# A second scheduling fence per step in the first phase of a fused attention and gated-layer kernel on one Trainium2 core

## The chip, the cores and the metric

The kernel runs on one core of one Trainium2 chip. The metric is the device time of one execution in microseconds (us), as the median of several runs. A core has TensorE (PE in the profile), VectorE (DVE), ScalarE (ACT), GpSimd (POOL) and SyncE (SP), which here issues nearly all DMAs. Each engine takes its instructions strictly in the order in which they were written for it, and waits at the head of its queue until the semaphores that an instruction names have been raised.

## What is computed

Three layers follow one another, over 4 batches of 576 positions:

```python
# 1: 8 heads of 64, causal within a window of 128
scores = q @ k.T / 8 + slope[h] * -|i - j|;  attn = softmax(masked scores);  x = attn @ v      # 576 x 512
# 2: gated layer with a spatial product
h = relu(x @ w_in);  u, v = h[:, :512], h[:, 512:]
v_n = (v - mean(v)) / sqrt(var(v) + 1e-6)
x = (u * (w_spatial @ v_n + b_spatial)) @ w_out
# 3: four causal attention experts of width 64, of which the best two by x @ w_gate are summed with softmaxed gates
```

Products that need more precision than one rounded operand gives are done in three passes over a high and a low part of each operand. The low part is the source less its rounded high part.

## The kernel before

**Two phases.** The first phase (lines 161 to 639) does layer 1 and the parts of layer 2 up to the gate. The second phase (from line 641) folds `w_out` into the weights of layer 3 and does layer 3. The change touches the first phase alone.

**Tiles and steps.** `tiles` (line 527) lists 20 tiles (b, j): batch b and 128 positions j, the fifth of 64. The loop of lines 605 to 635 makes 20 steps, s = 2 to 21; each works on several tiles at different stages. In step s PE makes the attention result `px` of tile s-2 (`attend`, line 402) and the scores of tile s (`scores`, line 341), and then, in pieces between other matmuls, the transposes of the probabilities of tile s-1 (`transposes`, line 383). ACT and DVE make the softmax of tile s (`softmax`, line 359; its exponentials are L151, its reduction L150). Names in this text carry batch and position: `px0_3` is batch 0, position 3.

**The eviction of x.** `take` (line 419) moves `px` from PSUM into the operand x of layer 2: `split` (line 131) rounds it into the high part on ACT (L132) and subtracts on DVE for the low part (L129). The pool `psT` (line 110) holds one buffer, shared by `px` and by the transposes `pt`, so the first transpose of a step has to wait until both halves of that step's eviction have read `px`.

**Work between.** `dense.pull` (line 76) hands PE pieces of layer 2 of earlier tiles: `v_tile` (`pv`, L436), `u_half` (`pu`, L499) and `spatial` (`pg`, L516 and L521). Their followers on ACT and DVE are the ReLU `vr` (L444), its statistics (L447, L448, L462 to L469), the normalisation (L472), the high part `vn0_t` (ACT, L475, and L482 for a half tile) and low part `vn1_t` (DVE, L129). POOL fills the padding of the last `vn0` tile after that (L483). The PSUM pool `psD` has three buffers for these.

**Other work that the loop spreads out.** `late_chunks` (line 549) decodes the last four pieces of `w_in` in steps 2 to 5; its word operations are L281 on ACT and L284 to L289 on DVE. `setup` (line 247) loads and splits the spatial weights in steps 6 to 8: a load into `st_wsp` (two buffers of tag `f64w`), an ACT cast (L254) and a DVE subtraction (L129). `out_weights` (line 291) decodes `w_out` from step 9 on (L281, L284 to L289, L308, cast `ho` L313, low part `lo`). `load_chunk` (line 324) loads q, k and v for two steps ahead; v has five buffers, so a v load waits on SP for the attention that reads the oldest one. After the loop, `load_wcat` (line 666) loads pieces of the third layer's weights into `st_wc`, in the same two buffers of tag `f64w`.

**What sets the order.** PE's order is that of the code, written by hand (line 1059: a manual schedule for PE). The order of ACT, DVE, POOL and SP is chosen while the program is built, by a scheduler with a timeline of its own. The one means that the code has over it is `tc.no_sync_barrier()` (line 608), a fence that no instruction passes in that ordering, on any engine; it emits no instruction and no semaphore. Each step has one, at its head:

```python
        tc.no_sync_barrier()
        if s == 9:
            early_stack.close()
            outw = out_weights(right.enter_context(...))
        if s > 2:
            b, j = tiles[s - 2]
            if j in (0, 2) and b > 0:
                dense.through(f"u{b - 1}_{j // 2}")
            px = attend(b, j)
        if s < len(tiles):
            scores(*tiles[s])
        if s > 2:
            take(*tiles[s - 2], px)
        if 4 <= s + 2 < len(tiles):
            load_chunk(*tiles[s + 2])
        now[0] += 1
        dense.pull(RATE / 6)
        parts(s)
```

The rest of a step (lines 626 to 635) is twice: `transposes`, `dense.pull`, `softmax`, `dense.pull`, `parts`.

Of the kernel before, what the change touches and what calls it, by code (L numbers as in the profile page):

```python
# [102 lines left out]
def block_kernel(ctx, tc, qP, kP, v, w_in, wspT, bsp, w_outT, wcat, wo, rel, relt, low, tri, out):  # L103
# [27 lines left out]
    def split(hi, lo, src):  # L131
        nc.scalar.copy(hi, src)  # L132
        lo_part(lo, src, hi)
# [157 lines left out]
    def out_weights(pool):  # L291

        is64 = w_outT.dtype == I64

        def load(k):
            raw = pool.tile([P, 512], w_outT.dtype, tag="raw", name=f"rawo{k}", bufs=2)
            nc.sync.dma_start(raw, w_outT[k * P : (k + 1) * P, :])
            return raw

        nxt = load(0)  # L300
        yield
        for k in range(4):
            w = nxt
            if is64:
                w = pool.tile([P, 512], F32, tag="w", name=f"wo{k}", bufs=2)
                f = pool.tile([P, 512], F32, tag="f", name=f"fo{k}", bufs=3)
                yield from word_bits(w, f, nxt, f)
                nc.vector.tensor_add(w, w, f)  # L308
            yield
            if k < 3:  # L310
                nxt = load(k + 1)
            hi = pool.tile([P, 512], F32R, tag="f", name=f"ho{k}", bufs=3)
            nc.scalar.copy(hi, w)  # L313
            nc.sync.dma_start(wt_dram[0, k], hi.bitcast(F32))
            yield
            lo = pool.tile([P, 512], F32R, tag="f", name=f"lo{k}", bufs=3)
            lo_part(lo, w, hi)
            nc.sync.dma_start(wt_dram[1, k], lo.bitcast(F32))
            yield
            yield  # L320
# [3 lines left out]
    def load_chunk(b, j):  # L324

        q0, qn = TOK[j]
        Q_[b, j] = a1.tile([P, 4, P], F32, tag="q", name=f"q{b}_{j}", bufs=3)
        nc.sync.dma_start(Q_[b, j], qP[b, :, j])
        if j == 0:
            K_[b] = a1.tile([P, 4, S], F32, tag="k", name=f"k{b}")  # L330
        if b == 0:
            nc.sync.dma_start(K_[b][:, :, q0 : q0 + qn], kP[b, :, :, q0 : q0 + qn])
        elif j == 0:
            nc.sync.dma_start(K_[b], kP[b])
        V_[b, j] = a1.tile([P, 512], F32, tag="v", name=f"v{b}_{j}", bufs=5)
        nc.sync.dma_start(V_[b, j][:qn], v[b, q0 : q0 + qn])
# [4 lines left out]
    def scores(b, j):  # L341

        q0, qn = TOK[j]
        k0 = max(0, q0 - P)
        kn = min(S, q0 + P) - k0
        for g in range(2):
            ps = psS.tile([P, 2, 512], F32, tag="S", name=f"ps{b}_{j}_{g}")
            for h in range(2):
                hp = 2 * g + h
                if j < 4:  # L350
                    for o in range(2):
                        r = slice(64 * o, 64 * o + 64)
                        nc.tensor.matmul(ps[:, o, 256 * h : 256 * h + kn], Q_[b, j][r, hp, :], K_[b][r, hp, k0 : k0 + kn], start=True, stop=True)  # L353
                else:

                    nc.tensor.matmul(ps[:, h, :kn], Q_[b, j][:, hp, :], K_[b][:, hp, k0 : k0 + kn], start=True, stop=True)
            st_[b, j, g] = ps

    def softmax(b, j, g):

        ps = st_[b, j, g]
        p = a1.tile([P, 4, P], F32, tag="p", name=f"p{b}_{j}_{g}", bufs=3)
        st = a1.tile([P, 8], F32, tag="stat", name=f"st{b}_{j}_{g}", bufs=4)
        if j == 4:
            nc.vector.copy_predicated(ps[:, :, 0:64], lowm[:, 128:192].unsqueeze(1).to_broadcast([P, 2, 64]), ps[:, :, 128:192])
            for h in range(2):
                row_softmax(p[:, h, :], ps[:, h, 0:P], reltail[:, 2 * g + h, :], st[:, h : h + 1], st[:, 4 + h : 5 + h])
            n = 2
        else:
            view = ps.rearrange("p o (h c) -> p (o h) c", h=2)  # L370
            if j > 0:
                nc.vector.copy_predicated(view[:, :, 0:P], lowm[:, 0:P].unsqueeze(1).to_broadcast([P, 4, P]), view[:, :, P:256])
            for i in range(4):
                o, h = i // 2, i % 2
                row_softmax(p[:, 2 * h + o, :], view[:, i, 0:P], relm[:, min(j, 1), 2 * (2 * g + h) + o, :], st[:, i : i + 1], st[:, 4 + 2 * h + o : 5 + 2 * h + o])
            n = 4
        sm = st[:, 4 : 4 + n]
        nc.vector.tensor_scalar(sm, sm, 1e-9, None, op0=ALU.add)
        nc.vector.reciprocal(sm, sm)
        nc.vector.tensor_tensor(p[:, :n, :], p[:, :n, :], sm.unsqueeze(2).to_broadcast([P, n, P]), op=ALU.mult)  # L380
        st_[b, j, g] = p

    def transposes(b, j, g):
        p = st_[b, j, g]
        n = 4 if j < 4 else 2
        pt = psT.tile([P, 4, P], F32, tag="T", name=f"pt{b}_{j}_{g}")
        here = a1.tile([P, 4, P], F32, tag="pT", name=f"pT{b}_{j}_{g}", bufs=4)
        before = None
        for i in range(n):
            nc.tensor.transpose(pt[:, i, :], p[:, i, :], ident)  # L390
        nc.scalar.copy(here[:, :n], pt[:, :n])  # L391
        if j > 0:

            before = a1.tile([P, 4, P], F32, tag="pU", name=f"pU{b}_{j}_{g}", bufs=4)
            w = P if j < 4 else 64
            m = 4
            u_, h = (t[:, :n].rearrange("p i (o q) -> p (i o) q", q=w) for t in (before, here))
            nc.gpsimd.affine_select(out=u_, in_=h, pattern=[[0, m], [-1, w]], compare_op=ALU.is_gt, fill=0.0, base=0, channel_multiplier=1)  # L398
            nc.gpsimd.affine_select(out=h[:w], in_=h[:w], pattern=[[0, m], [1, w]], compare_op=ALU.is_ge, fill=0.0, base=0, channel_multiplier=-1)  # L399
        st_[b, j, g] = (before, here)  # L400

    def attend(b, j):

        q0, qn = TOK[j]
        px = psT.tile([P, 4, P], F32, tag="T", name=f"px{b}_{j}")
        for hp in range(4):
            pT = st_[b, j, hp // 2]
            for t, w in ((j - 1, pT[0]), (j, pT[1])):
                if t < 0:
                    continue  # L410
                kb = TOK[t][1]
                for o in range(2):
                    h = 2 * hp + o
                    rhs = w[:, 2 * (hp % 2) + o, :] if j < 4 else w[:kb, hp % 2, 64 * o : 64 * o + 64]
                    nc.tensor.matmul(px[64 * o : 64 * o + 64, hp, :qn], V_[b, t][:kb, h * 64 : h * 64 + 64], rhs,  # L415
                                     start=(t == max(0, j - 1)), stop=(t == j))
        return px

    def take(b, j, px):
        q0, qn = TOK[j]  # L420
        if j < 4:
            split(x[0][:, :, q0 : q0 + P], x[1][:, :, q0 : q0 + P], px)
        else:
            twice = [t[:, :, 512:640].rearrange("p m (r c) -> p m r c", r=2) for t in x]
            split(*twice, px[:, :, :64].unsqueeze(2).to_broadcast([P, 4, 2, 64]))
        xready[b, j] = now[0] + (b == 0)
# [133 lines left out]
    def parts(s):  # L560

        next(late, None)
        for _ in range(2 if 6 <= s < 9 else 0):
            next(prep, None)
        if s >= 9:
            next(outw, None)
# [38 lines left out]
    for s in range(2, len(tiles) + 2):  # L605
        now[0] = 4 * s
# [4 lines that stand above are left out]
            outw = out_weights(right.enter_context(tc.tile_pool(name="later", bufs=1, side="right")))  # L611
# [6 lines that stand above are left out]
            scores(*tiles[s])  # L618
        if s > 2:
            take(*tiles[s - 2], px)  # L620
        if 4 <= s + 2 < len(tiles):
            load_chunk(*tiles[s + 2])
        now[0] += 1
        dense.pull(RATE / 6)
        parts(s)
        for g in range(2):
            if 1 <= s <= len(tiles):
                transposes(*tiles[s - 1], g)
            dense.pull(RATE / 6)
            if s < len(tiles):  # L630
                softmax(*tiles[s], g)
# [4 lines that stand above are left out]
# [427 lines left out]
```

## Time and profile before

| | |
|---|---|
| median of 3 runs | 510.27 us (509.82 to 510.5) |
| span of the profiled execution, first to last instruction | 508.8 us |
| its own time | not listed apart; the median is 1.5 us over its span |
| first phase, up to the last `pg` | 0 to 298 us |
| PE busy | 486.7 us, 96% |
| DVE, ACT, POOL busy | 308.4, 261.3, 98.2 us (61%, 51%, 19%) |
| DMA | 44.34 MB, 87 GB/s over the span |
| mean granted TensorE clock | 0.989 |

A row of the timeline gives the start in us from the span's start, the duration, engine, line, operation and tiles (buffer numbers left out), how many were merged, and in brackets the time that the engine sat idle before it, with what ended that. PEld is PE's loading of weights, beside its matmuls; SPq is SP's issuing of DMAs. A granted clock of 1.00 is 2.4 GHz and 0.50 is 1.2 GHz.

### The profile page before, as it was taken

What the parts mean: (1) busy time and instruction counts of PE and PEld (TensorE: products, weight loads), DVE (VectorE), ACT (ScalarE), POOL (GpSimd) and SP (SyncE); (2) the same over time, 40 slices, a digit from 0 to 9 for tenths busy, and PEclk for the clock granted to TensorE, in tenths of its full rate; (3) what the DMA queues carried; (4) which work ended last, traced back from release to release, by engine and by line L of the source; (5) the groups of instructions that cost most, each with busy time, mean ns of one, the idle gap of its engine ahead of it and who ended that gap; (6) DMA issues with size and microseconds to landing.
All of it is one profiled execution on the core that took longest, in us unless ns stands there. A gap on an engine that the chain in (4) does not pass through costs nothing.

```text
span 508.8 us, 10533 instructions
## 1 busy us (share of the span) xinstructions
PE 486.7 (96%) x3910; PEld 425.1 (84%) x3910; DVE 308.4 (61%) x1069; ACT 261.3 (51%) x778; POOL 98.2 (19%) x205
## 2 busy tenths in 40 slices
PE   8879889999999999999999999999999999999995
PEld 6547668898988988899887999998899899897783
DVE  4978868655787766785463723455484565555431
ACT  4765457533666436473353513355575555545563
POOL 0012210222101222111112010103322243232131
PEclk9999979999999999999999999999999999999999
DMA  8931223215321451201304660311000000002231
GB/s 286 371 133 43 65 87 103 115 69 168 107 95 43 181 191 43 95 2 48 110 1 125 224 204 1 94 63 32 1 22 3 2 22 1 1 1 84 84 104 63
DMA packets 25063, 44.34 MB, mean 87 GB/s; under 512 B 5810, under 2 KB 8242, under 8 KB 24628
## 3 DMA queue, kind: packets, MB, share of 16 engines
q1 hardware_dynamic: 24868, 43.54, 25.3%
q8 instruction: 31, 0.51, 0.4%
q14 instruction: 20, 0.16, 0.1%
q10 hardware_dynamic: 144, 0.13, 0.1%
HBM read 32.13 MB, written 11.53 MB: 86 GB/s over the span
## 4 chain that ended last, share of the span: by engine, by line
PE 77%; DVE 10%; ACT 6%; DMA 4%; issue 1%; SPq 1%; ACTq 0%
PE pg L516 10%; PE pv L436 10%; PE pq L780 10%; PE pu L499 6%; PE pvB L804 6%; PE pxB L906 5%; PE pout L927 5%; PE px L415 4%; PE ptB L888 4%; PE psB L845 4%; PE pw L679 3%; PE ps L353 3%; PE pt L390 2%; ACT p L151 2%; PE pg L521 2%; DMA raw<-in_w_in 2%
## 5 line engine op out<-in xcount | busy, mean ns | idle before, releaser
L151 ACT ACTIVATE p<-p,st 128x128 f32<-128x128 f32 x144 | 56.3, 392 | 37.6 <-DVE st L150 37.6
L436 PE MATMUL pv<-win,x 128*128 128x512 f32 x240 | 64.8, 413 | 0.7 <-ACT x L132 0.7
L780 PE MATMUL pq<-x,W 128*128 128x288 f32 x384 | 58.3, 302 | 0.8 <-DVE k L129 0.8
L516 PE MATMUL pg<-wsp,vn 128*128 128x288 f32 x384 | 58.9, 298 | 0.1
L398 POOL TENSOR_SCALAR_AFFINE_SELECT pU<-pT 128x512 f32<-128x512 f32 (+1 forms) x32 | 22.9, 715 | 168.7 <-ACT pT L391 164.7
L499 PE MATMUL pu<-x,win 128*128 128x288 f32 x384 | 55.2, 298 | 0.0
L780 PEld LDWEIGHTS pq<-x,W 128*128 128x128 f32 x384 | 52.0, 188 | 3.6 <-DVE k L129 1.5
L158 POOL TENSOR_SCALAR pB<-pB,stB 128x128 f32<-128x128 f32 (+4 forms) x72 | 39.1, 562 | 78.8 <-DVE stB L868 62.4
L516 PEld LDWEIGHTS pg<-wsp,vn 128*128 128x128 f32 x384 | 52.9, 188 | 1.3 <-issue 1.0
L499 PEld LDWEIGHTS pu<-x,win 128*128 128x128 f32 x384 | 52.0, 188 | 1.9 <-issue 0.5
L436 PEld LDWEIGHTS pv<-win,x 128*128 128x128 f32 x240 | 44.6, 195 | 10.0 <-issue 1.0
L151 ACT ACTIVATE pB<-pB,stB 128x128 f32<-128x128 f32 (+3 forms) x64 | 35.7, 559 | 21.4 <-DVE stB L150 21.4
L150 DVE CUSTOM_DVE_ANT_0 pB<-psB,trit 128x128 f32<-128x128 f32 (+3 forms) x64 | 28.2, 486 | 9.9 <-PE psB L845 9.2
L804 PE MATMUL pvB<-W,x 128*128 128x260 f32 (+1 forms) x240 | 34.2, 289 | 0.0
L927 PE MATMUL pout<-wo,o 128*128 128x512 f32 x108 | 30.8, 411 | 0.9 <-ACT o L132 0.9
L804 PEld LDWEIGHTS pvB<-W,x 128*128 128x128 f32 (+1 forms) x240 | 29.9, 178 | 1.7 <-issue 1.7
L888 PE MATMUL ptB<-ident,pB 128*128 128x128 f32 (+1 forms) x200 | 30.7, 273 | 0.0
L390 PE MATMUL pt<-ident,p 128*128 128x128 f32 x144 | 23.2, 280 | 7.6 <-DVE x L129 6.0
L150 DVE CUSTOM_DVE_ANT_0 p<-ps,relm 128x128 f32<-128x128 f32 x128 | 29.5, 285 | 0.7 <-DMA relm<-in_rel 0.2
L906 PE MATMUL pxB<-pTB,vt 128*64 128x128 f32 (+2 forms) x480 | 28.3, 262 | 1.4 <-ACT pTB L889 1.4
L415 PE MATMUL px<-pT,v 128*64 128x128 f32 (+1 forms) x320 | 29.4, 274 | 0.3 <-POOL pT L399 0.3
L353 PE MATMUL ps<-k,q 64*128 64x256 f32 (+1 forms) x256 | 28.6, 363 | 0.6 <-DMA k<-in_kP 0.6
(147 smaller groups left out, 875.6 us busy)
## 6 DMA issues: line engine op xcount, KB each, us to landing
q<-in_qP SPq DMA_DIRECT2D x20, 256.0 KB, 2.9
g_dram<-g SPq DMA_DIRECT2D x16, 288.0 KB, 2.1
raw<-in_w_in SPq DMA_DIRECT2D x8, 512.0 KB, 6.8
v<-in_v SPq DMA_DIRECT2D x16, 256.0 KB, 3.4
gf<-g_dram SPq DMA_DIRECT2D x4, 1024.0 KB, 5.5
out<-ot SPq DMA_DIRECT2D x15, 256.0 KB, 2.0
k<-in_kP SPq DMA_DIRECT2D x3, 1152.0 KB, 5.3
rawo<-in_w_outT SPq DMA_DIRECT2D x4, 512.0 KB, 4.2
```

The lines of the kernel that those rows point to most:

```text
L150: nc.vector.tensor_tensor_reduce(s_view, ps_view, tab, -0.125, FLT_MAX, ALU.add, ALU.min, nm)
L151: nc.scalar.activation(s_view, s_view, AF.Exp, bias=nm, scale=-1.0, accum_out=sm)
L353: nc.tensor.matmul(ps[:, o, 256 * h : 256 * h + kn], Q_[b, j][r, hp, :], K_[b][r, hp, k0 : k0 + kn], start=True, stop=True)
L415: nc.tensor.matmul(px[64 * o : 64 * o + 64, hp, :qn], V_[b, t][:kb, h * 64 : h * 64 + 64], rhs, start=(t == max(0, j - 1)), stop=(t == j))
L436: nc.tensor.matmul(pv, x[i][:, k, t0 : t0 + P], win[j][:, k, 512:1024], start=(n == 0), stop=(n == 11))
L499: nc.tensor.matmul(pu[:, :HALF], win[i][:, k, m * P : (m + 1) * P], x[j][:, k, c], start=(n == 0), stop=(n == 11))
L516: nc.tensor.matmul(pg[:, :HALF], vn[i][k][:, m * P : (m + 1) * P], wsp[j][:, k, c], start=(n == 0), stop=False)
L780: nc.tensor.matmul(pq[:, :HALF], W[i][:, k, c0 : c0 + P], G[j][:, k, c], start=(n == 0), stop=(n == 11))
L804: nc.tensor.matmul(pv[:tn, :260], G[i][:, k, COL[t] : COL[t] + tn], W[j][:, k, 512:772], start=(n == 0), stop=(n == 11))
L888: nc.tensor.transpose(pt[:kb, n, :], p[pr][:, o, c0 : c0 + kb], ident)
L906: nc.tensor.matmul(px[64 * o : 64 * o + 64, pr, :qn], vt[:kb, c, (2 * pr + o) * 64 : (2 * pr + o) * 64 + 64], rhs, start=(c == 0), stop=(c ...
L927: nc.tensor.matmul(po[:tn], o2[i][:, pr, :tn], wos[j][:, pr, :], start=(n == 0), stop=(n == 5))
```

## The change

After `take`, a step now has a second fence. What was written before it (the step's attention, scores and eviction of x, and all of earlier steps) can no longer be ordered behind what is written after it (the loads for two steps ahead, the dense pieces' followers, decoding, transposes and softmax), and the other way round.

```diff
@@ -618,6 +618,7 @@
             scores(*tiles[s])
         if s > 2:
             take(*tiles[s - 2], px)
+            tc.no_sync_barrier()
         if 4 <= s + 2 < len(tiles):
             load_chunk(*tiles[s + 2])
         now[0] += 1
```

No instruction is added or removed. PE's and POOL's orders are the same as before, instruction by instruction. DVE's, ACT's and SP's differ, in the first phase and up to the splitting of `st_wc`; the second phase's are the same from the first `pw` on. Line numbers in the orders of the changed kernel are higher by one from line 621 on.

DVE in step 5, from the statistics of `v_tile` to the softmax of tile (1, 0): `vr0_t` is normalised, `vn1_t` is its low part, `x1` the low part of x. Before:

```order
L469 TENSOR_TENSOR vs0_422<-vs0_422 128x3
L472 TENSOR_SCALAR vr0_0_423<-vr0_0_423,vs0_422 128x512
L472 TENSOR_SCALAR vr0_1_572<-vr0_1_572,vs0_422 128x512
L472 TENSOR_SCALAR vr0_2_679<-vr0_2_679,vs0_422 128x512
L129 TENSOR_TENSOR vn1_0_115<-vr0_0_423,vn0_0_110 128x512
L129 TENSOR_TENSOR vn1_1_116<-vr0_1_572,vn0_1_111 128x512
L129 TENSOR_TENSOR vn1_2_117<-vr0_2_679,vn0_2_112 128x512
L129 TENSOR_TENSOR x1_105<-px0_3_702,x0_104 128x4x128
```

And now:

```order
L469 TENSOR_TENSOR vs0_422<-vs0_422 128x3
L472 TENSOR_SCALAR vr0_0_423<-vr0_0_423,vs0_422 128x512
L129 TENSOR_TENSOR x1_105<-px0_3_704,x0_104 128x4x128
L472 TENSOR_SCALAR vr0_1_573<-vr0_1_573,vs0_422 128x512
L472 TENSOR_SCALAR vr0_2_681<-vr0_2_681,vs0_422 128x512
```

The low part of x stands ahead of five operations that stood ahead of it.

SP's DMA issues between steps 5 and 7 (`v1_3` is the v load of tile (1, 3), `st_wsp` the spatial weights). Before:

```order
L328 DMA q1_3_832<-in_qP 128x512
L252 DMA st_wsp0_836<-in_wspT 128x576
L252 DMA st_wsp1_839<-in_wspT 128x576
L336 DMA v1_3_834<-in_v 128x512
L252 DMA st_wsp2_873<-in_wspT 128x576
```

And now:

```order
L328 DMA q1_3_836<-in_qP 128x512
L336 DMA v1_3_838<-in_v 128x512
L252 DMA st_wsp0_840<-in_wspT 128x576
L252 DMA st_wsp1_843<-in_wspT 128x576
L252 DMA st_wsp2_877<-in_wspT 128x576
```

The two first loads of spatial weights went behind the v load. On ACT the cast of `st_wsp0` stands in both kernels right behind the x of `px0_4`, ahead of the exponentials of tile (1, 1).

ACT behind the last tile's eviction, at the end of the first phase. Before:

```order
L132 CAST x0_104<-px3_4_3139 128x4x128
L132 CAST wc00_3279<-st_wc0_3287 128x772
L132 CAST wc01_3280<-st_wc1_3289 128x772
L444 ACTIVATE vr3_4_3171<-pv3_4_3158 128x512
L503 ACTIVATE u0_106<-pu3_0_1_3177 128x288
L462 ACTIVATE vs3_2909<-vs3_2909,eps_81 128x2
L463 ACTIVATE vs3_2909<-vs3_2909 128x2
L503 ACTIVATE u1_107<-pu3_1_1_3197 128x288
L475 CAST vn0_3_113<-vr3_3_3134 128x512
```

And now:

```order
L132 CAST x0_104<-px3_4_3157 128x4x128
L444 ACTIVATE vr3_4_3190<-pv3_4_3177 128x512
L462 ACTIVATE vs3_2925<-vs3_2925,eps_81 128x2
L503 ACTIVATE u0_106<-pu3_0_1_3196 128x288
L463 ACTIVATE vs3_2925<-vs3_2925 128x2
L503 ACTIVATE u1_107<-pu3_1_1_3216 128x288
L132 CAST wc00_3298<-st_wc0_3306 128x772
L475 CAST vn0_3_113<-vr3_3_3152 128x512
```

The cast of `st_wc0` went behind the ReLU pieces and stands right ahead of `vn0_3`. On DVE its subtraction likewise went to just ahead of `vn1_3`. On SP the loads of `st_wc0` and `st_wc1`, which stood ahead of the loads of `trit`, `tritail` and the eight pieces of `wt`, now stand behind these ten.

## Rows read from the trace of the kernel before

**Rows 1.** Who waited for whom, PE: us in total, times, longest us.

```profile
PE pt L390 <- DVE x L129: 6.0, 5, 3.7
```

**Rows 2.** Timeline of PE, step 5 and into step 6: start, us, what, idle before.

```profile
60.88 1.16 PE L353 MATMUL ps<-k,q 64*128 64x128 f32 x16
65.78 0.69 PE L390 MATMUL pt<-ident,p 128*128 128x128 f32 x2 [3.73 <-DVE x L129]
66.12 3.76 PE L436 MATMUL pv<-win,x 128*128 128x512 f32 x8
...
71.70 0.34 PE L415 MATMUL px<-pU,v 128*64 128x64 f32 x4
```

**Rows 3.** Timeline of DVE and ACT, step 5.

```profile
61.86 1.46 DVE L472 TENSOR_SCALAR vr<-vr,vs 128x512 f32<-128x512 f32 x3
...
62.44 1.14 ACT L475 CAST vn<-vr 128x512 fp32r<-128x512 f32 x2 [1.42 <-DVE vr L472]
...
63.23 1.89 DVE L129 TENSOR_TENSOR vn<-vr,vn 128x512 fp32r<-128x512 f32 x3
...
65.04 0.68 DVE L129 TENSOR_TENSOR x<-px,x 128x512 fp32r<-128x512 f32 x1
```

**Rows 4.** Busy time by stretch: PE, PEld, DVE, ACT, POOL, granted clock, DMA share, GB/s.

```profile
33.00:37.20 4.20, 1.44 (x7) 0.63 (x5) 4.20 (x17) 3.33 (x14) 1.55 (x2) 1.00 0.29 120
37.20:40.70 3.50, 2.89 (x28) 2.92 (x30) 3.36 (x10) 1.05 (x3) 1.27 (x2) 0.51 0.00 0
...
64.50:71.40 6.90, 5.62 (x16) 4.44 (x16) 5.02 (x25) 3.91 (x19) 1.32 (x4) 0.51 0.26 92
```

**Rows 5.** The page, part 5: busy us, mean ns of one, then idle before.

```profile
L151 ACT ACTIVATE p<-p,st 128x128 f32<-128x128 f32 x144 | 56.3, 392 | 37.6 <-DVE st L150 37.6
```

**Rows 6.** Timeline of SP's DMA issues, with one row of ACT, steps 5 to 7.

```profile
62.96 0.94 SPq L252 DMA_DIRECT2D st_wsp<-in_wspT  x2
...
73.66 0.33 SPq L336 DMA_DIRECT2D v<-in_v  x1
...
76.53 5.41 SPq L252 DMA_DIRECT2D st_wsp<-in_wspT  x4
...
79.31 0.67 ACT L254 CAST wsp<-st_wsp 128x576 fp32r<-128x576 f32 x1 [0.44 <-DMA st_wsp<-in_wspT]
```

**Rows 7.** Timeline of PE, step 6.

```profile
76.15 2.09 PE L436 MATMUL pv<-win,x 128*128 128x512 f32 x8
78.53 0.65 PE L390 MATMUL pt<-ident,p 128*128 128x128 f32 x4 [0.29 <-ACT pT L391]
```

**Rows 8.** Timeline of DVE, step 10, and of ACT and PE, step 12.

```profile
130.33 0.69 DVE L129 TENSOR_TENSOR x<-px,x 128x512 fp32r<-128x512 f32 x1 [0.52 <-ACT x L132]
...
159.38 0.62 ACT L313 CAST ho<-wo 128x512 fp32r<-128x512 f32 x1 [2.22 <-DVE wo L308]
...
162.79 0.66 PE L390 MATMUL pt<-ident,p 128*128 128x128 f32 x4 [0.63 <-ACT pT L391]
```

**Rows 9.** Timeline of PE, step 20.

```profile
266.20 0.44 PE L390 MATMUL pt<-ident,p 128*128 128x128 f32 x2 [0.89 <-DVE x L129]
```

**Rows 10.** Timeline of all engines, end of the first phase.

```profile
277.55 1.07 SPq L668 DMA_DIRECT2D st_wc<-in_wcat  x2
...
283.13 0.62 POOL L483 TENSOR_SCALAR vn<-pad 33x512 fp32r<-33x512 f32 x1 [9.80 <-DVE vn L129]
283.26 1.74 PE L516 MATMUL pg<-wsp,vn 128*128 128x288 f32 x12
283.63 0.84 ACT L132 CAST wc<-st_wc 128x772 fp32r<-128x772 f32 x1 [0.76 <-DMA st_wc<-in_wcat]
...
284.50 0.96 DVE L129 TENSOR_TENSOR wc<-st_wc,wc 128x772 fp32r<-128x772 f32 x1 [1.53 <-ACT wc L132]
...
284.84 0.43 PE L521 MATMUL pg<-wsp,vn 97*128 97x288 f32 x2
```

**Rows 11.** The page, part 6: DMA issues, KB each, median us from issue to landing.

```profile
st_wc<-in_wcat SPq DMA_DIRECT2D x4, 386.0 KB, 4.9
```

## The prediction

> **What bounds the kernel now.** I read the rows of who waited for whom first, then the timelines around the longest of these waits, then the granted clock by stretch. PE is busy nearly all the time, so what can be won or lost in the first phase is PE's idle time and PE's time at the lower clock. The wait that the change aims at is there: PE's transposes waited 6.0 us in five places for the low part of x on DVE, 3.7 us of it once [rows 1]. That one is step 5. PE has ended the scores at 62.04 and gets its next instruction, the first transpose, at 65.78 [rows 2]: the single buffer of transposes and attention result is free only when the low part of x has been taken. On DVE that operation stood behind three normalisations (1.46 us) and three low parts (1.89 us), which need nothing of it [rows 3].
>
> The idle time cost more than itself. In the stretch from 64.50 to 71.40 the granted clock was 0.51, the lower of the two levels (1.2 GHz), after PE had idled 3.73 us; it was 0.51 also from 37.20 to 40.70, after a stretch in which PE was busy 1.44 of 4.20 us [rows 4]. Eight matmuls `pv` took 3.76 us at that level [rows 2] and 2.09 us at the full one [rows 7].
>
> **The change part by part.** No instruction comes or goes, and PE's order stays, so every term below is a shift of PE's starts: what PE gains or loses in a stage, carried on to the next. Negative is faster.
>
> *Step 5: -3.6.* Now one normalisation stands ahead of x instead of six operations. ACT has room for its half, since it idled 1.42 us until 62.44 [rows 3] with the attention done at 60.9. One normalisation is a third of 1.46, so DVE starts x at 61.86 + 0.49 = 62.35, and with 0.68 for it PE goes on at 63.1 instead of 65.78: 2.7 us. PE would also run the rest of the step at the full clock. What stood between 65.78 and the next attention at 71.70, 5.9 us, would shrink to about 3.3, but then another engine is late: the second copy of transposed probabilities on ACT, which that attention needs, stands behind five exponentials at 0.39 each [rows 5]. They cannot start before the casts of the normalised tiles, pushed to about 65.0. 65.0 + 1.95 + 0.4 for the copy and 0.7 for POOL's masking and the handing over is 68.1. So the attention starts 71.7 - 68.1 = 3.6 us earlier.
>
> *Step 6: +1.7, and +0.6 behind it.* Here SP's new order bites. The v load waits on SP for exactly this attention (it was issued at 73.66, as the attention ended), and the two loads of spatial weights, issued at 62.96 before, now stand behind it [rows 6]. They are 3.6 us early with the attention: v at 70.06, the first weight load at about 70.5. A load of this kind landed at 79.3 after its issue at 76.53, 2.75 us [rows 6]; so it lands at 73.2. On ACT its cast stands at the head of step 6, ahead of four exponentials and the copy of the first transposes, for which the second transposes on PE wait. Cast 0.67 [rows 6], three exponentials 1.2, second cast 0.6, a fourth exponential 0.4, copy 0.6: 76.65. Before, that PE wait ended at 78.53 after 0.29 us [rows 7]. 1.9 us of the lead is left, 1.7 are gone, and PE, done with its `pv` at 78.24 - 3.6 = 74.6, idles 2.0 us. The later loads of the same two buffers hang one behind the other, and ACT's casts of them now stall in front of the evictions of `pu`; I put 0.6 us on this, between 0 (the buffers cover it) and 1.9 (all that is left).
>
> *Steps 2 to 4: 0.* Decoding of `w_in`, five DVE operations, goes from in front of x, where it filled DVE's waiting, to behind it among the softmax. Of the 6.0 us of waits some 1.4 lie outside steps 5 and 20 [rows 1, 2, 9] and could be won; five operations of at most 0.69 us, as a DVE subtraction of this size takes [rows 8], are 3.4 that could be lost. The softmax has a step to spare, so I take 0.
>
> *Steps 9 to 12: +1.3.* The same for `w_out`. In step 10 DVE waited only 0.52 us for x, because decoding filled the time ahead of it [rows 8]; now three such operations go behind x, among the reductions. In step 12 ACT waited 2.22 us for this decoding before the cast `ho`, which stands ahead of the exponentials and the copy on which PE then waited 0.63 us [rows 8]. DVE and ACT are thus late there already, and nothing makes them earlier: a PE that arrives 1.3 us early waits 1.3 us longer. Bounds: 0, if they follow the lead, and 1.9. I take 1.3, since PE's wait there shows no slack.
>
> *Steps 13 to 20: -0.9.* In step 20 PE waited 0.89 us for x [rows 9], which is now ahead of the work that delayed it. Bounds 0 and 1.4.
>
> *End of the phase: +2.5.* The weight loads `st_wc0` and `st_wc1` now stand behind ten others on SP, in the place that `st_wc2` had: issued at 277.55, landed by 283.61, where ACT had waited 0.76 us for it [rows 10]. Then it hurt nobody, as `vn0_3`, `vn0_4` and `vn1_4` were done. Now the cast of `st_wc0` stands ahead of these. From 283.63: cast 0.84, DVE's subtraction of it ends at 285.46; then `vn1_3` and `vn1_4`, 0.65 each, 286.7; POOL's padding 0.62 and 0.1 to hand over, 287.4. The matmul that reads it started at 284.84 [rows 10]. That is 2.5 us, in two pieces, the first for `vn0_3`. Everything here hangs on the end of the last attention, so it shifts with it and the difference stays. Bounds: 0.3, by the landing of a free load [rows 6], and 3.5, if the second cast holds `pu` too.
>
> The page DMA: Bandwidth & Descriptors of the Trainium skill (section Anatomy of one DMA) prices a transfer at 2.0 us and its bytes at 436 GB/s; for these 386 KB [rows 11] that is an estimate of 2.9 us, by which `st_wc0` would land at 280.5, this term would be near 0.3 and the sum 2.2 lower. The trace's 6.06 us behind eight other loads decides against it.
>
> *The clock: +1.7.* The new waits of PE, 2.0 us in step 6, about 1.9 in step 12 (0.63 and 1.3) and 2.5 in two pieces at the end, lie near the idle time that preceded the first fall, 2.8 us of 4.20 [rows 4]. A fall as short as that one, 3.5 us at half speed, costs 1.7 us. Between none and three falls (0 and 5.1) I take one.
>
> *Sum:* -3.6 + 1.7 + 0.6 + 0 + 1.3 - 0.9 + 2.5 + 1.7 = +3.3 us, so a span of 508.8 + 3.3 = 512.1. The profiled execution's own time is its span and an unlisted rest; with the 1.5 us by which the median of the runs is over the span, the forecast is 510.3 + 3.3 = 513.6 us. The second phase keeps its orders and hides nothing of this: PE is the bound there.
>
> **The rivals.**
>
> *The lead holds (faster).* One mechanism: ACT's early casts of spatial weights find their data landed. It decides at step 6: if the first weight load has landed when ACT is through with x of that step, about 2.5 us earlier than I reckon, and DVE and ACT carry the lead through step 12, -3.6 and -0.9 stand against the end's 2.5: -2.0, 508.3 us. For it: a PE wait of 3.73 us goes for certain. Against it: the v load cannot be issued earlier. The Trainium skill's page Perfetto Trace Analysis (section Optimization Strategies) advises to speed up whatever an idle matmul engine waits for, which is what the change does; by that advice alone the answer lies here or lower.
>
> *It cancels.* The clock never falls, and `st_wc0` lands in the 4.9 us that is the median of such loads [rows 11] instead of 6.06, so the end costs 1.3: -3.6 + 1.7 + 0.6 + 1.3 - 0.9 + 1.3 = +0.4, 510.7 us. For it: the only falls before followed longer idle times.
>
> *It does nothing.* The fence would order only what was ordered already. The orders speak against it: all three engines' differ.
>
> **How the numbers follow.** The forecast gets 0.73, the lead that holds 0.12, cancelling 0.13, nothing 0.02. About 0.2%, 1.0 us, is what a measurement of this kernel tells from no change. So faster has 0.12, same 0.15, slower 0.73. The forecast's own range runs from 511.5 (no fall, the smaller end) to 517.0 (two falls, whole costs). Down to 509.6 it takes in cancelling and leaves out most of the faster case; above 517.0 some 0.08 is left out.
>
> **What would show it.** Right: PE's transposes of step 5 wait about 1 us for x and the low clock behind them is gone; ACT waits for the `st_wsp` load before its first cast, and PE waits about 2 us for a copy on ACT in step 6; PE waits inside the first `pg` of batch 3 for `vn0_3` and then for POOL. Wrong: a first weight load that is issued before the v load; a first `pg` of batch 3 without idle time; a lead of PE over the old trace that is still there in steps 13 to 19; a clock that never falls after step 5.

## The result and the profile after

The changed kernel takes 515.55 us (median of 4 runs, 514.02 to 516.44), the kernel before beside it 510.38 us. The ratio is 1.0094, 95% interval 1.0072 to 1.0116: 5.2 us slower, where 3.3 were forecast. The profiled execution has a span of 514.5 us (508.8 before), PE busy 490.6 us, a mean granted clock of 0.983.

Who PE waited for, in the changed kernel (us in total, times, longest us):

```profile
PE px L415 <- ACT pT L391: 3.3, 2, 2.6
PE pt L390 <- ACT pT L391: 3.1, 3, 1.9
PE pg L521 <- POOL vn L483: 1.8, 1, 1.8
...
PE pg L516 <- ACT vn L475: 1.1, 1, 1.1
PE pt L390 <- DVE x L129: 1.0, 1, 1.0
...
PE psw L218 <- DVE u L286: 0.9, 1, 0.9
...
PE pu L499 <- ACT u L503: 0.8, 1, 0.8
```

The fence did what it says: the waits for x have fallen from 6.0 us in five places [rows 1] to 1.0 in one. (The five were 0.41 us in step 4, 3.73 in step 5, 0.65 in step 7, 0.28 in step 14 and 0.89 in step 20.) The other rows are waits that the kernel before did not have, or, in the first two rows, had smaller (2.6 and 1.6 us).

PE's timeline in steps 4 to 6, 12 and 20:

```profile
57.36 1.13 PE L218 MATMUL psw<-u,ident 128*128 128x512 f32 x2 [0.92 <-DVE u L286]
...
62.44 1.16 PE L353 MATMUL ps<-k,q 64*128 64x128 f32 x16
64.61 0.44 PE L390 MATMUL pt<-ident,p 128*128 128x128 f32 x2 [1.01 <-DVE x L129]
64.80 2.10 PE L436 MATMUL pv<-win,x 128*128 128x512 f32 x8
...
68.79 0.34 PE L415 MATMUL px<-pU,v 128*64 128x64 f32 x4 [0.74 <-ACT pT L391]
...
70.89 3.56 PE L353 MATMUL ps<-k,q 64*128 64x256 f32 x16
...
77.39 0.66 PE L390 MATMUL pt<-ident,p 128*128 128x128 f32 x4 [0.43 <-ACT pT L391]
...
163.03 0.88 PE L390 MATMUL pt<-ident,p 128*128 128x128 f32 x4 [1.94 <-ACT pT L391]
...
266.51 0.38 PE L390 MATMUL pt<-ident,p 128*128 128x128 f32 x2
```

Step 5 waits 1.01 us instead of 3.73, its `pv` run at the full clock (2.10 us against 3.76 [rows 2]), and the attention of step 6 starts at 68.79 against 71.70. Step 20's wait of 0.89 [rows 9] is gone; step 12's grew from 0.63 [rows 8] to 1.94. The scores of step 6 took 3.56 us: the clock had fallen. The windows show where it was low (PE, PEld, DVE, ACT, POOL, granted clock, DMA share, GB/s):

```profile
37.20:40.70 3.50, 2.84 (x28) 2.87 (x29) 2.40 (x7) 0.52 (x2) 1.28 (x2) 0.50 0.00 0
40.70:44.00 3.30, 3.30 (x20) 2.54 (x19) 1.42 (x3) 1.16 (x2) 0.00 (x0) 0.52 0.34 84
64.50:70.80 6.30, 5.45 (x48) 4.10 (x48) 6.16 (x28) 5.35 (x22) 2.13 (x4) 1.00 0.16 44
71.00:74.40 3.40, 3.40 (x17) 2.27 (x17) 3.25 (x13) 0.92 (x2) 0.00 (x0) 0.52 0.67 232
163.20:166.60 3.40, 3.40 (x17) 3.40 (x17) 2.69 (x6) 2.48 (x12) 1.97 (x4) 0.52 0.15 56
289.70:293.10 3.40, 3.40 (x16) 3.40 (x16) 2.42 (x5) 2.32 (x4) 0.00 (x0) 0.51 0.23 90
```

The stretch behind step 5's wait [rows 4] is at the full clock now. Three new stretches of 3.4 us at the lower level stand behind the waits of steps 5, 12 and the end, and the first fall, which lasted 3.5 us before [rows 4], lasts 6.8.

SP and ACT in step 6, where the v load now stands ahead of the weight loads:

```profile
70.74 0.33 SPq L336 DMA_DIRECT2D v<-in_v  x1
71.12 10.31 SPq L252 DMA_DIRECT2D st_wsp<-in_wspT  x6
...
74.06 0.67 ACT L254 CAST wsp<-st_wsp 128x576 fp32r<-128x576 f32 x1 [2.47 <-DMA st_wsp<-in_wspT]
```

ACT waits 2.47 us for the first load, as predicted; PE waits only 0.43 for what comes of it, since the fall of the clock just before had made PE itself late.

The end of the phase, all engines:

```profile
278.30 0.92 SPq L669 DMA_DIRECT2D st_wc<-in_wcat  x2
...
283.81 0.83 ACT L132 CAST wc<-st_wc 128x772 fp32r<-128x772 f32 x1 [2.86 <-DMA st_wc<-in_wcat]
284.55 1.14 ACT L475 CAST vn<-vr 128x512 fp32r<-128x512 f32 x2
...
285.22 1.47 PE L516 MATMUL pg<-wsp,vn 128*128 128x288 f32 x9 [1.13 <-ACT vn L475]
...
287.13 1.31 POOL L483 TENSOR_SCALAR vn<-pad 33x512 fp32r<-33x512 f32 x1 [13.51 <-DVE vn L129]
...
288.49 0.54 PE L521 MATMUL pg<-wsp,vn 97*128 97x288 f32 x2 [1.80 <-POOL vn L483]
```

ACT stands 2.86 us at the split of `st_wc0`; `vn0_3` is cast behind it, and PE waits 1.13 us for that and 1.80 for POOL. Before, the matmul at 288.49 started at 284.84 [rows 10].

Followed matmul by matmul, PE's lag behind the trace of before runs: +1.6 us into step 5 (most of it the longer first fall), -2.9 at the attention of step 6, -1.4 after the fall there, -1.1 from step 7 on, +1.8 after step 12 and its fall, +0.3 behind step 20, +5.3 at the start of the fold.

These are one execution of each kernel, and the clock differs from one to the next. The four of the changed kernel took 516.19 and 516.44 us at a mean granted clock of 0.983, 514.91 at 0.990 and 514.02 at 0.993. Over all measurements the kernel before took 510.24 to 511.59 us at 0.990 and 509.36 to 509.80 at 0.992 and 0.993. At about the same clock the change is still some 4 us slower, so the clock alone is not the loss.

### The profile page after: what moved, and what is told of

Its sections match the earlier page's. It is cut to its first block, busy times and chain, and to the rows that moved or that the text cites. A ratio compares the mean times of both kernels' runs of the same rounds, so it can differ in the third digit from the quotient of the medians.

```text
span 514.5 us, 10541 instructions
## 1 busy us (share of the span) xinstructions
PE 490.6 (95%) x3910; PEld 428.4 (83%) x3910; DVE 306.6 (60%) x1069; ACT 259.9 (51%) x778; POOL 99.3 (19%) x205
## 4 chain that ended last, share of the span: by engine, by line
PE 77%; DVE 7%; ACT 5%; DMA 5%; issue 2%; SPq 2%; POOL 0%; ACTq 0%; POOLq 0%; DVEq 0%
PE pg L516 10%; PE pq L781 10%; PE pv L436 7%; PE pu L499 7%; PE px L415 6%; PE pvB L805 5%; PE pout L928 5%; PE pxB L907 5%; PE ptB L889 4%; PE psB L846 4%; PE pw L680 3%; PE ps L353 3%; PE pt L390 2%; ACT p L151 2%; PE pg L521 2%
## 5 line engine op out<-in xcount | busy, mean ns | idle before, releaser
L436 PE MATMUL pv<-win,x 128*128 128x512 f32 x240 | 62.4, 402 | 0.7 <-ACT x L132 0.7
L516 PE MATMUL pg<-wsp,vn 128*128 128x288 f32 x384 | 61.7, 307 | 1.1 <-ACT vn L475 1.1
L516 PEld LDWEIGHTS pg<-wsp,vn 128*128 128x128 f32 x384 | 55.7, 197 | 2.4 <-ACT vn L475 1.4
L436 PEld LDWEIGHTS pv<-win,x 128*128 128x128 f32 x240 | 43.0, 188 | 9.6 <-issue 1.0
L129 DVE TENSOR_TENSOR x<-px,x 128x512 fp32r<-128x512 f32 x20 | 13.8, 689 | 33.8 <-ACT x L132 33.7
L132 ACT CAST x<-px 128x512 fp32r<-128x512 f32 x20 | 11.7, 584 | 41.3 <-PE px L415 41.3
L353 PE MATMUL ps<-k,q 64*128 64x256 f32 (+1 forms) x256 | 31.3, 388 | 0.7 <-DMA k<-in_kP 0.7
```

Of the source, the lines that this page charges most:

```text
L436: nc.tensor.matmul(pv, x[i][:, k, t0 : t0 + P], win[j][:, k, 512:1024], start=(n == 0), stop=(n == 11))
L516: nc.tensor.matmul(pg[:, :HALF], vn[i][k][:, m * P : (m + 1) * P], wsp[j][:, k, c], start=(n == 0), stop=False)
```

## The experiments

**e1: no second fence in the last step.**

```diff
             take(*tiles[s - 2], px)
-            tc.no_sync_barrier()
+            if s < 21:
+                tc.no_sync_barrier()
```

> The second fence in every step but the last (s = 21), so that the loads of st_wc0 and st_wc1 stand again ahead of the ten others on SP. Theory A (the loss sits in separate places, and the largest is the order at the end): the 2.9 us in which PE waited for vn0_3 and for POOL, and the 2.1 us that the lower clock cost behind them, both go: 515.5 - 5.0 = 510.5 us, the profile equal to that of the change up to 283 us. Theory B (the loss is low-clock time that comes and goes from one execution to the next, as the first fall shows, 3.4 us long before and 6.8 after with the same start): no clear gain, 514 to 516 us, and PE goes on waiting or loses the time later. Theory C (the end is all there is to it, the other shifts cancel): 510.5 us as well.

Measured: 512.87 us, ratio to before 1.0061 (1.0037 to 1.0085). `st_wc0` and `st_wc1` are loaded early again and split at once, and still PE waits. ACT and PE at the end of the phase:

```profile
282.12 0.83 ACT L132 CAST wc<-st_wc 128x772 fp32r<-128x772 f32 x1 [4.41 <-DMA st_wc<-in_wcat]
282.86 0.40 ACT L503 ACTIVATE u<-pu 128x288 f32<-128x288 f32 x1
283.16 0.61 ACT L475 CAST vn<-vr 128x512 fp32r<-128x512 f32 x1
...
283.32 1.96 PE L516 MATMUL pg<-wsp,vn 128*128 128x288 f32 x12 [1.52 <-ACT u L503]
...
287.06 0.54 PE L521 MATMUL pg<-wsp,vn 97*128 97x288 f32 x2 [1.79 <-POOL vn L483]
```

It is `st_wc2` now that ACT stands at, for 4.41 us, in front of a piece of u and of `vn0_3`. The wait has changed its tile and hardly its size (1.52 + 1.79 us). By the medians about half of theory A's gain came, 2.7 us. In the trace little of it is the end's: PE's lag grows there by 4.1 us, against 5.0 in the change, where a fall of the clock took 1.6 of it. Here no fall came. None came behind the wait of 1.95 us in step 12 either; from there to the end of the phase the granted clock was 1.00:

```profile
162.00:290.00 128.00, 123.32 (x990) 111.14 (x991) 80.25 (x268) 62.40 (x194) 23.68 (x40) 1.00 0.29 101
```

So this run does not say what the fence of the last step costs.

**e2: no second fence in steps 9 to 12.**

```diff
             take(*tiles[s - 2], px)
-            tc.no_sync_barrier()
+            if not 9 <= s <= 12:
+                tc.no_sync_barrier()
```

> The second fence in all steps but 9 to 12, so that the decoding of w_out stands again ahead of x on DVE. Theory A: the wait of 1.94 us of PE in step 12 and the fall of the clock behind it (1.5 us) were made by the decoding pushed into the softmax. Without it PE's transposes of tile (2, 1) start at about 162.8 us as before, or at 161.7 if the lead of 1.07 us holds: 515.5 - 1.8 = 513.7 to 515.5 - 2.9 = 612.6 - 100 = 512.6 us. Theory B: 514 to 516 us. Theory C (the shifts of the middle cancel, the end is all): 515.5 us.

(The "612.6 - 100" in it is a slip for 512.6.) Measured: 507.66 us, ratio 0.9958 (0.9939 to 0.9977), 7.9 us below the change where A expected 1.8 to 2.9. Step 12 waits 0.63 us again. By the two traces step 12 with its fall gives 2.9 us of it and a shorter first fall 1.4. The rest, 3.4, came from a place that nobody had expected, the end. PE, SP and ACT:

```profile
75.99 0.65 PE L390 MATMUL pt<-ident,p 128*128 128x128 f32 x4 [2.11 <-ACT pT L391]
...
160.29 0.66 PE L390 MATMUL pt<-ident,p 128*128 128x128 f32 x4 [0.63 <-ACT pT L391]
...
273.63 1.11 SPq L670 DMA_DIRECT2D st_wc<-in_wcat  x2
...
278.49 1.14 ACT L475 CAST vn<-vr 128x512 fp32r<-128x512 f32 x2 [0.24 <-DVE vr L472]
279.54 0.62 ACT L482 CAST vn<-vr 64x512 fp32r<-64x512 f32 x1
280.06 0.40 ACT L503 ACTIVATE u<-pu 128x288 f32<-128x288 f32 x1
280.36 1.56 ACT L132 CAST wc<-st_wc 128x772 fp32r<-128x772 f32 x2
```

The loads of `st_wc0` and `st_wc1` stand as late as in the change, behind the ten others. But their casts stand behind `vn0_3` and `vn0_4`, and PE has no wait in the first `pg`. So leaving out fences over 100 us earlier moved an order at the end. That it went by way of the scheduler's own timeline is my reading; no run shows it by itself.

**e3: no second fence in steps 3 and 4.**

```diff
             take(*tiles[s - 2], px)
-            tc.no_sync_barrier()
+            if s > 4:
+                tc.no_sync_barrier()
```

> The second fence from step 5 on. Theory A: the wait of 0.9 us of PE in step 4 for the decoding of w_in, and 0.6 us behind it, go, the old waits for x of 0.4 and 0.3 us come back: PE starts step 5 about 1.5 us earlier than in the change. Step 6 hangs on the v load behind PE's attention, so all of this may be carried on: 514.0 us, or 514.8 if half is lost in step 6. Theory B: 514 to 516 us with no place of its own. Theory C: 515.5 us.

Measured: 513.55 us, ratio 1.0076 (1.0053 to 1.0099). The wait of 0.9 us for the decoding is gone, the old waits of step 4 are back (0.20 us for POOL's masking and 0.41 for x; 0.26 and 0.41 in the kernel before), and all later waits of the change are there: 1.94 us in step 12, 1.70 and 1.79 in the first `pg`. By the medians somewhat more came than A had, 2.0 us, but the runs of either kernel spread over 2.3 us or more. Executions of the same mean granted clock lie 0.6 to 0.9 us apart: 515.50 us against 516.19 and 516.44 at 0.983, 513.18 and 513.37 against 514.02 at 0.993. That is A with half lost on the way.

**e4: the second fence in steps 5 to 8 and 13 to 20.**

```diff
             take(*tiles[s - 2], px)
-            tc.no_sync_barrier()
+            if 5 <= s <= 8 or 13 <= s <= 20:
+                tc.no_sync_barrier()
```

> The second fence in steps 5 to 8 and 13 to 20 alone: the places where theory A has its gains, without the three where it has its losses (w_in in steps 3 and 4, w_out in 9 to 12, st_wc at the end). Theory A: 515.5 - 5.0 for the end - 1.8 to 2.9 for step 12 - 0 to 1.5 for step 4: 506.1 to 508.7 us, faster than before; 509 to 510 if step 12 takes the lead back, as it did not depend on PE in the kernel before. Theory B: 510 to 516 us, by chance. Theory C: 510.5 us, as before.

Measured: 508.19 us, ratio 0.9957 (0.994 to 0.9973), in theory A's range. The end has before's order and no wait; step 12 waits 0.63 us, and PE's lead is 1.6 us ahead of it and behind it.

**e5: the second fence in step 5 alone.**

```diff
             take(*tiles[s - 2], px)
-            tc.no_sync_barrier()
+            if s == 5:
+                tc.no_sync_barrier()
```

> The second fence in step 5 alone. SP's order and the end of the phase are those of the kernel before; on ACT and DVE only the work around steps 5 and 6 moves. Theory A (each place has its own price, and PE's lead is carried through step 12, where the runs showed the same wait of 0.63 us at leads of 1.5 to 2.4 us): PE starts the attention of step 6 some 3.9 us earlier, and with the weight loads ahead of the v load it loses 0.3 us at most in step 6, so 510.2 - 3.9 + 0.3 = 506.6 us, 506 to 507.4 with the changes of the clock. Theory D (the prediction's step: what is won ahead of step 12 is waited for in step 12): 509.5 to 510.2 us, with a wait of 2 us or more of PE in step 12.

Measured: 509.99 us, ratio 0.9991 (0.9977 to 1.0004). The number is D's and the place is not: step 12 waits 0.63 us. Nearly all of the lead of 4.4 us is lost in step 6. ACT and PE there:

```profile
74.71 0.67 ACT L254 CAST wsp<-st_wsp 128x576 fp32r<-128x576 f32 x1 [0.65 <-DMA st_wsp<-in_wspT]
...
76.45 0.65 ACT L254 CAST wsp<-st_wsp 128x576 fp32r<-128x576 f32 x1
77.02 0.57 ACT L391 COPY pT<-pt 128x512 f32<-128x512 f32 x1
...
77.64 0.66 PE L390 MATMUL pt<-ident,p 128*128 128x128 f32 x4 [3.76 <-ACT pT L391]
```

With the weight loads ahead of the v load the scheduler put the third and the fourth weight cast in front of the copy that PE waits for, and the third waits for its load, which had to wait for a buffer; on DVE two weight subtractions of 0.7 us stand ahead of the scores' mask. A's "0.3 us at most in step 6" was wrong: the price of step 6 is that of ACT's and DVE's orders, whichever load is late.

**e6: the second fence in steps 9 to 12 alone.**

```diff
             take(*tiles[s - 2], px)
-            tc.no_sync_barrier()
+            if 9 <= s <= 12:
+                tc.no_sync_barrier()
```

> The second fence in steps 9 to 12 alone. Theory A: the decoding of w_out goes into the softmax, PE waits 1.94 us instead of 0.63 in step 12: 510.2 + 1.3 = 511.5 us, 513.2 with one fall of the clock behind the wait; and since the order at the end also comes out otherwise (the cast of st_wc2 stands ahead of vn0_4), up to 1.5 us more there: 511.5 to 514.7 us. Theory E (these fences harm only together with the lead that the others make): 510.2 us, a wait of 0.6 us in step 12.

Measured: 512.27 us, ratio 1.0035 (1.0021 to 1.0048): these four fences are harmful by themselves. Step 12 waits 1.04 us, between the two theories: here DVE has the second half's mask (L372, 0.69 us) behind the first half's reductions, in the change it stands ahead of them. At the end one cast, of `st_wc2`, stands in front of `vn0_4`; PE waits 0.29 us for POOL there. In its trace these two places cost 0.4 and 0.5 us; a third loss, 1.6 us, is a stretch at the lower clock from 274.4 us on, behind the wait of 0.69 us for the last x, which the kernel before has as well, without a fall.

**e7: the change, with the splits of st_wc0 and st_wc1 behind vn.**

```diff
     later = deque([load_wcat(0), load_wcat(1)])
-    for k in (2, 3):
-        dense.pull(1000.0)
-        later.popleft()()
-        later.append(load_wcat(k))
+    dense.pull(2000.0)
     dense.through("u3_1")
+    dense.flush()
+    tc.no_sync_barrier()
+    for k in (2, 3):
+        later.popleft()()
+        later.append(load_wcat(k))
```

> The change, with the splits of st_wc0 and st_wc1 written behind the last u piece and a third fence ahead of them: the loads stay where the change has them, behind the ten others on SP, but on ACT and DVE the splits stand behind vn0_3, vn0_4, vn1_3 and vn1_4. Theory A (the place of the splits in ACT's and DVE's orders costs, not the late load): the 2.9 us of waits in the first pg of batch 3 go, and the fall behind them: 515.5 - 2.9 = 512.6 to 515.5 - 5.0 = 510.5 us, with no wait of PE for vn0_3 or POOL. Theory F (the load that lands late costs by itself): 515 us, PE waits later, in the fold, for the weights.

Measured: 509.47 us, ratio 0.9976 (0.9962 to 0.999): 6.1 us below the change, by one edit at the end. SP, ACT and PE there:

```profile
276.77 1.05 SPq L669 DMA_DIRECT2D st_wc<-in_wcat  x2
...
279.97 1.14 ACT L475 CAST vn<-vr 128x512 fp32r<-128x512 f32 x2
...
283.00 1.66 ACT L132 CAST wc<-st_wc 128x772 fp32r<-128x772 f32 x2
...
282.49 1.74 PE L516 MATMUL pg<-wsp,vn 128*128 128x288 f32 x12
284.07 0.43 PE L521 MATMUL pg<-wsp,vn 97*128 97x288 f32 x2
```

The loads are late, ACT doesn't stand at them, PE doesn't wait, and no fall of the clock follows. Theory F falls: late loads cost nothing as long as nothing urgent stands behind their casts. By the two traces, of the 6.1 us 3.4 are the end's waits and what came with them and 1.6 the fall there; the other 1.0 is PE's earlier arrival at the end, and is there already in step 5, behind a shorter first fall. In the kernel before, the casts of `st_wc0` and `st_wc1` stand further ahead than in the change, right behind the last x, and with landed data they cost nothing: it takes both, late data and something urgent behind its cast.

**e8 and e9: the fences of e2, and the first two weight loads ahead of the v load.**

```diff
+        if s == 6:
+            for k in (0, 1):
+                early_wsp[k] = load_wsp(k)
         if s > 2:
             take(*tiles[s - 2], px)
...
             dense.pull(RATE / 6)
+            if s == 6:
+                tc.no_sync_barrier()
             parts(s)
```

`load_wsp` holds the two lines of `spatial_weights` that make the tile and issue its load; the third fence keeps the later weight casts behind the first half's exponentials.

> The fences of e2 (all steps but 9 to 12), and the two first loads of spatial weights issued ahead of the second fence of step 6, so ahead of the v load, with one more fence that keeps the later casts behind the first half's exponentials. Theory A (step 6 costs 1.8 us because ACT's first cast waits for a weight load that waits behind the v load): PE's wait of 2.11 us before the transposes of tile (1, 0)'s second half falls to 0.3 or so: 507.7 - 1.8 = 505.9 us. Theory G (the exponentials or the second x are late there anyway): the wait stays at 2 us or turns up a few us later, 507.7 us.

Measured: a ratio of 0.9996 (0.9977 to 1.0014), where e2 had 0.9958: no gain over e2, but a loss of some 2 us by the ratios. To see where, the same kernel ran once more.

> The kernel of e8 once more, for a profile that shows where its time went (e8 came out at 510.6 us, 3 us above e2, where theory A had 505.9). Theory A, mended: the late weight load is no longer what PE waits for in step 6, but the third fence there holds back the softmax of the second half, so that PE waits about 2 us or more for the copy of the second half's transposes at the start of step 7 or ahead of it; the end is free of waits as in e2. Theory G: PE's wait of 2.1 us before the transposes of the second half of tile (1, 0) is still there.

Measured: 509.93 us, ratio 1.0004 (0.9991 to 1.0017). PE and ACT (its lines are higher by seven):

```profile
75.69 0.60 PE L397 MATMUL pt<-ident,p 128*128 128x128 f32 x4
...
88.23 0.68 ACT L261 CAST wsp<-st_wsp 128x576 fp32r<-128x576 f32 x1 [2.56 <-DMA st_wsp<-in_wspT]
...
91.79 0.44 PE L397 MATMUL pt<-ident,p 128*128 128x128 f32 x2 [2.36 <-DVE x L129]
```

ACT's first cast finds its data, and PE has no wait left in step 6, as theory A said. How much of the 2.1 us that is worth stays open, since in this trace the clock fell there (3.4 us from 69.75 on), which had left only 0.43 of the wait in the change too. The time is lost again in step 7, by another way than the mended theory had it: the fifth weight load gets its buffer only after an earlier split has read it, ACT stands 2.56 us at its cast, and x of step 7 is behind that. The five loads share two buffers; what is gained at the first is here asked for at the last.

**e10: no second fence in steps 3, 4 and 9 to 12.**

```diff
             take(*tiles[s - 2], px)
-            tc.no_sync_barrier()
+            if 5 <= s <= 8 or s >= 13:
+                tc.no_sync_barrier()
```

> The second fence in steps 5 to 8 and from 13 on: e2 without the fences of steps 3 and 4. On ACT the splits of st_wc0 and st_wc1 stand behind all u pieces and vn, as in e7. Theory A: step 4's wait of 0.9 us for the decoding is gone, the 0.6 us of old waits for x in steps 3 and 4 are back, all else as in e2: 507.7 - 0.9 + 0.6 = 507.4 us, 506.5 to 508.2 with one more or one less stretch at the lower clock; no wait of PE of over 0.3 us from step 13 to the last pg but the 0.69 for the last x. Theory C' (the order at the end decides all): as e2 and e4, 507.7 to 508.2 us.

Measured: 506.68 us (506.49 to 507.96), ratio 0.9939 (0.9923 to 0.9956). It beats both kernels: 3.4 us below before, 8.9 below the change. Who PE waited for in it:

```profile
PE pt L390 <- ACT pT L391: 3.6, 3, 2.2
...
PE pt L390 <- DVE x L129: 1.4, 2, 1.0
...
PE pv L436 <- ACT x L132: 0.7, 1, 0.7
PE pu L499 <- ACT u L503: 0.7, 1, 0.7
```

From step 13 to the fold only the 0.7 us for the last x is left; the 2.2 us are step 6.

## Why the prediction was right

The direction and the places were right, the sum was 1.9 us too small (5.2 against 3.3). By the two traces (5.3 us at the start of the fold) the clock cost 3.0 us more than its term, PE was 1.6 late into step 5, for which there was no term, and the other terms together came out 2.6 us lower.

- *Step 5, -3.6.* Measured -4.5 (lag +1.6 to -2.9 at the attention of step 6; e5 has +0.1 to -4.4). The wait fell by 2.72 us where 2.7 were worked out. The rest of the step was mis-sized by 0.9: from the end of the scores to the next attention I had 6.1 us (62.04 to 68.1), set by ACT's exponentials and copy; the trace has 5.2 (63.60 to 68.79), with 0.74 of it waiting for that copy.
- *Step 6, +1.7.* Right, but hidden in the changed kernel. Where the clock did not fall just before, PE waits 2.11 us (e2) and 2.21 (e10) where 2.0 were predicted, and loses 1.8 and 1.9 us of its lead. In the change the fall came first: 1.6 us lost to the clock, 0.2 to the wait.
- *Behind it, +0.6.* PE lost 1.2 us among the `pu` of step 6, 0.76 of it waiting for an eviction of u on ACT. In step 7 it got 1.1 back, most of it the wait of 0.65 us for x that the trace of before has there, which I had put among the 0 of steps 2 to 4.
- *Steps 2 to 4, 0.* Nearly right: 0.9 us of waiting for the decoding of `w_in` came, and a wait of 0.41 for x and one of 0.26 for POOL's masking went, both in step 4. Of the 1.4 us that I set against the loss here only the 0.41 lay here; 0.65 were step 7's and 0.28 step 14's. Where the first fall was short, PE enters step 5 at a lag of +0.1 to +0.5 us with the fences (e2, e7, e9) and of 0.0 to +0.1 without (e5, e6, e10). Where it was long, it is +1.1 and +1.6 with them (e1, the change), +0.5 and +0.8 without (e3, e4).
- *Steps 9 to 12, +1.3.* The number is right (0.63 to 1.94 us), **the step behind it failed**: "a PE that arrives 1.3 us early waits 1.3 us longer". With leads of 0.7 (e5) to 2.5 us (e2) e2, e4, e5 and e10 wait 0.63 us; with the fences in place the change, e1, e3 and e7 wait 1.94 or 1.95, whatever their lead (1.1 to 2.1 us). DVE and ACT do follow PE, and the orders of the softmax are what costs: with the decoding alone behind x, e6 waits 1.04 us; where the second half's mask stands ahead of the first half's reductions as well, it is 1.94. The lead was not lost there.
- *Steps 13 to 20, -0.9.* Measured -1.5: 1.1 in step 20 and 0.4 in step 14, where a wait of 0.28 went.
- *End, +2.5.* Measured 3.4 us (lag +0.3 to +3.7 at the matmul of 284.84), 2.93 of it in the two waits named. Of the 0.9 too little, 0.7 is POOL's padding, which took 1.31 us where I had 0.62. e7 shows that the place of the splits is the cause. The late load alone costs nothing (e2, e7).
- *The clock, +1.7.* This is the term that was most mis-sized. Measured 4.7 us in three falls of which I took one: 1.6 us behind the waits of 1.01 and 0.74 us of step 5, a step earlier than I had it, 1.5 behind step 12, 1.6 at the end. The 1.6 us into step 5 come on top, most of them the longer first fall; e3 and e4 had that fall too, without the fences of steps 3 and 4. All this is the account of one execution. Those of the change at a clock of 0.990 and 0.993 instead of 0.983 were only 1.3 to 2.4 us faster: where a fall does not come, part of its time can be lost in a wait instead, as in step 6.

The rival "the lead holds" needed the first weight load to be there in time; it was issued 0.4 us behind the v load, and ACT stood 2.47 us. In e9 the load was there in time and the lead was lost all the same, in step 7. The rival "it cancels" needed a `st_wc` load of 4.9 us and no fall: the load took up to 5.5 us (278.30 to 283.81), and the clock fell.

The Trainium skill's page DMA: Bandwidth & Descriptors (section Anatomy of one DMA) states its 2.0 us and 436 GB/s for transfers that GpSimd issues. SP issues these, so the 2.9 us for that load was an estimate from a neighbouring case; the trace has up to 5.5 with eight loads issued just ahead of it. For a spatial weight load of 288 KB the same sum would be 2.7 us, an estimate as well, and the trace has 2.75 [rows 6]. The Trainium skill's page Perfetto Trace Analysis (section Optimization Strategies) advises to speed up what an idle PE waits for. That wait did go, and the kernel was slower: here the advice paid only where the order that it brought cost less elsewhere than it won, as in e10, which still waits 2.2 us in step 6.

## What to carry to other kernels

A scheduling fence is no local edit: it moves every loose operation to one side, and, as e2 shows, orders of stages far behind it as well. Try it step by step, and read the orders of all queues up to the end of the phase each time: a long wait alone does not tell where it pays, since e5, with the fence only in the step of the longest wait, gained nothing. On an engine that works in order, look for a cast or copy of data still on its way that stands in front of something that PE needs; in these runs late loads hurt there and nowhere else.

## What the runs showed of the hardware

Kernels in which PE stood within 0.3 us of one another at 35 us had a first stretch at the lower clock of 3.4 us (before, e2, e5 to e7, e9, e10) or of 6.8 (the change, e1, e3, e4). A wait of 2.11 us in step 6 was followed by no fall in e2, one of 2.12 us in e4 by a fall at 78.0. The waits of 1.94 us in step 12 and of 1.13 and 1.80 at the end were each followed by a fall in the change; in e1 waits of 1.95, 1.52 and 1.79 in the same places were not. The wait of 0.69 us for the last x was followed by a fall in e2 (at 270.3) and in e6 (at 274.4), and in no other trace. So whether a wait costs its length, or its length and some 1.6 us, can't be said of one execution. The runs of one kernel spread by this: in e2 the span was 505.2 to 505.4 us at a mean granted clock of 0.996, and 507.9 at 0.987.
